# Attention and mixture of experts on one core: six of batch 1's ten k'q steps are called later, in pairs beside the first three expert blocks

## The chip, the cores and the metric

The kernel runs on one core of a Trainium2 chip. The core has five engines with a queue each, and each queue is worked off in order: PE (matrix multiply, with its weight loads shown as PEld), DVE (elementwise work of two operands, reductions), ACT (functions of one operand, casts, copies), POOL (here memsets, a few tensor operations and the scatters, which are DMAs that it issues itself) and SP (which issues the other DMAs). The metric is the time of one execution in device microseconds (us). Before the change it was 1244.78 us, the median of three runs from 1243.62 to 1246.61.

## The reference

There are B = 4 batches of N = 5056 tokens with C = 256 channels.

```python
qn = q / (norm(q, axis=1) + 1e-6)          # per channel, over all tokens of a batch
kn = k / (norm(k, axis=1) + 1e-6)
s = kn.T @ qn / tau                        # 256 x 256 for each batch
a = softmax(s)
x = v @ a                                  # 20224 tokens of 256 channels
logits = x @ w_gate + modality_bias[modality_id]
e = argmax(logits)                         # one of 8 experts for each token
out[token] = gate * (relu(x @ w1[e]) @ w2[e])   # hidden size 1024
```

So a batch's attention matrix needs a sum over all of its tokens (k'q and the squared norms) before the first of its tokens can be multiplied with it, and an expert can only start when enough tokens have been routed to it.

## The kernel before, in words

**Steps.** Each batch is cut into NS = 10 steps of 512 tokens (the last has 448), G = 40 steps in all, counted g = 0 to 39. Products in 32-bit floats are made from a high and a low part: ACT casts the high part, DVE subtracts to get the low part, and PE multiplies high by high, high by low and low by high.

**k'q** (`kq_pieces`, L218). A step of k'q has five pieces: load (L223), and for each half h of 256 tokens split (L250) and mm (L276). split makes two casts on ACT (L257) and two subtractions on DVE (L258), and for the norms a square on ACT (L272) and an addition to `acc` on DVE (L274), for q and for k. mm makes 4 matmuls of 512 columns (L283) and 4 of 256 (L287). A step that stands in `SELF` takes its norm from 4 more matmuls in each half (`selfk`, L294) in place of squares and additions. For batch 1's k these are steps 0 to 3 before the change.

**Routing** (`va_pieces`, L431). For step g: load of v (L443), transposes of v (L460) with their high and low parts (L464, L465), the product with the attention matrix (L476, copied out at L480), and `route` (L482): the logits, the largest of them, a running count of tokens for each expert (L507, L512 to L514), the row number `pi` of each token (L528), and four scatters of x into the sorted array `xs` (L407, on POOL). From g = 3 on `pick` (L556 to L581) chooses the rows and the expert of one block for each step; its result is `pki` (L579).

**Blocks** (`block_pieces`, L588). A block is 512 rows of one expert: SP reads `pki`, loads the weights (L615, L619, four DMAs of 512 KB) and the rows (`xr`, L596, which waits until the scatters of steps 0 to g have landed); ACT and DVE split the weights (L634, L635); PE transposes xr (L645) and makes the two layers (`hp`, L663, and `y`, L683). The block chosen after step g runs beside step g + 4. So steps g = 0 to 6 have no block beside them, the first block runs beside g = 7, and from then on each step has one.

**The order.** The loop at L768 calls, for each g, the pieces of up to three streams in turn (`_interleave`, L20): the block's, the routing's (with the next step's v, and the softmax ahead of a batch's first step), and the next batch's k'q, one step beside each g. The order in which pieces are called is a priority only: the framework then plans an order for each engine by its own estimate of the times, and may put an instruction ahead of others whose inputs come later. The trace shows how far: the memset of `modi` (L182) that is called after g = 15 runs at 95.99 us, amid the scatters of g = 2 and 3. What limits such moves is buffers. A tag of a pool has as many buffers as the pool says (p2: two, p3: three), and an instruction that needs one waits for the last use of the tile that had it.

**Buffers of k'q.** Inputs q and k have two buffers each in p2. Batch 1's steps 2, 3 and 4 borrow the three-deep buffers of the blocks' weights (`w1r`, `w2r`) as long as no block runs, the second halves of steps 0 to 3 borrow `xh` and `xl`, and their squares `hh` and `hl`.

Of the kernel before, what the change touches and what calls it, by code (L numbers as in the profile page):

```python
# [18 lines left out]

def _interleave(*streams):  # L20

    lists = [list(s) for s in streams if s]
    total = [len(x) for x in lists]
    at = [0] * len(lists)
    while any(a < n for a, n in zip(at, total)):
        i = min(
            (i for i in range(len(lists)) if at[i] < total[i]),
            key=lambda i: ((at[i] + 0.5) / total[i], i),
        )
        lists[i][at[i]]()  # L30
        at[i] += 1
# [3 lines left out]
def kernel(  # L35
# [20 lines left out]
    NS = -(-N // STEP)  # L56
# [15 lines left out]

    SELF = {
        "q": [{1, 4, 7}, set(), set(), set()],
        "k": [set(range(NS)), set(range(4)), set(), set()],
    }
    START = 3

    def parts(s):
        return P if s < NS - 1 else PL  # L80
# [137 lines left out]
    def kq_pieces(b, s):  # L218
        pp = parts(s)
        st = {}  # L220
        t0 = s * STEP

        def load():  # L223
            if s == 0:
                gram[b] = [
                    ps1.tile([P, 2 * C], F32, tag=f"{'y' if b == 0 else 'g'}{m}", name=f"g{m}_{b}")
                    for m in range(CH)
                ]
                acc[b] = p1.tile([P, 2, 2 * C], F32, tag="acc", name=f"acc_{b}", bufs=2)
                for n in ("k", "q"):  # L230
                    if SELF[n][b]:
                        selfp[n, b] = ps2.tile([P, CH, 2 * P], F32, tag="h", name=f"self{n}_{b}")
                        norm[n, b] = p1.tile([P, CH], F32, tag=f"n{n}", name=f"n{n}_{b}")
            for n, src, tag in (("q", q, "w1r"), ("k", k, "w2r")):
                if (b == 0 and s % 5 >= 2) or (b == 1 and 2 <= s < START + 2):
                    st[n] = p3.tile([P, TT, C], F32, tag=tag, name=f"{n}_{b}_{s}")
                else:
                    st[n] = p2.tile([P, TT, C], F32, tag=n, name=f"{n}_{b}_{s}")
                rows = src[b, t0 : t0 + pp * TT, :].rearrange("(p t) c -> p t c", t=TT)
                if b == 0 and s == 0:  # L240
                    st[n + "rows"] = rows
                else:
                    nc.sync.dma_start(st[n][:pp], rows)
            if b == 0 and s == 0:
                for h in range(2):
                    ts = slice(2 * h, 2 * h + 2)
                    for n in ("q", "k"):
                        nc.sync.dma_start(st[n][:, ts, :], st[n + "rows"][:, ts, :])

        def split(h):  # L250
            ts = slice(2 * h, 2 * h + 2)
            more = h == 1 and (b == 0 or (b == 1 and s < START + 1))
            qs = p2.tile([P, 2, 2 * C], F32R, tag="xh" if more else "qs", name=f"qs_{b}_{s}_{h}")
            ks = p2.tile([P, 2, 2 * C], F32R, tag="xl" if more else "ks", name=f"ks_{b}_{s}_{h}")
            st[h] = (qs, ks)
            for n, t in (("q", qs), ("k", ks)):
                nc.scalar.copy(t[:pp, :, 0:C], st[n][:pp, ts, :])  # L257
                nc.vector.tensor_tensor(  # L258
                    t[:pp, :, C : 2 * C], st[n][:pp, ts, :], t[:pp, :, 0:C].bitcast(F32), ALU.subtract
                )  # L260
            a = acc[b]
            for n, o in (("q", 0), ("k", C)):
                if s in SELF[n][b]:
                    continue
                first = h == 0 and s == min(set(range(NS)) - SELF[n][b])
                sq = a[:, :, o : o + C]
                if not first:
                    if b == 0 or (b == 1 and s < START + 1):
                        sq = p3.tile([P, 2, C], F32, tag="hh" if n == "q" else "hl", name=f"sq_{b}_{s}_{h}_{n}")
                    else:  # L270
                        sq = p2.tile([P, 2, C], F32, tag="sq", name=f"sq_{b}_{s}_{h}_{n}")
                nc.scalar.activation(sq[:pp], st[n][:pp, ts, :], AF.Square)  # L272
                if not first:
                    nc.vector.tensor_tensor(a[:pp, :, o : o + C], a[:pp, :, o : o + C], sq[:pp], ALU.add)  # L274

        def mm(h):  # L276
            qs, ks = st[h]
            for t in range(2):
                first = s == 0 and h == 0 and t == 0
                last = s == NS - 1 and h == 1 and t == 1  # L280
                for m in range(CH):
                    g = gram[b][m]
                    nc.tensor.matmul(  # L283
                        g, ks[:pp, t, m * P : (m + 1) * P], qs[:pp, t, :],
                        start=first, stop=False, skip_group_check=True,
                    )
                    nc.tensor.matmul(  # L287
                        g[:, 0:C], ks[:pp, t, C + m * P : C + (m + 1) * P], qs[:pp, t, 0:C],
                        start=False, stop=last, skip_group_check=True,
                    )  # L290
                    for n, x in (("k", ks), ("q", qs)):
                        mine = SELF[n][b]
                        if s in mine:
                            nc.tensor.matmul(  # L294
                                selfp[n, b][:, m, :], x[:pp, t, m * P : (m + 1) * P],
                                x[:pp, t, :].rearrange("p (s c) -> p s c", s=2)[:, :, m * P : (m + 1) * P],
                                start=s == min(mine) and h == 0 and t == 0 and m == 0,
                                stop=s == max(mine) and h == 1 and t == 1,
                                skip_group_check=True,
                            )  # L300
            for n in ("k", "q"):
                if h == 1 and SELF[n][b] and s == max(SELF[n][b]):

                    dg = p1.tile([P, 2 * P], F32, tag="sc", name=f"dg{n}_{b}", bufs=2)
                    for m in range(CH):
                        nc.vector.scalar_tensor_tensor(
                            dg, selfp[n, b][:, m, :], 1.0, ident12, ALU.mult, ALU.mult,
                            accum_out=norm[n, b][:, m : m + 1],
                        )

        yield load
        for h in range(2):
            yield lambda h=h: split(h)
            yield lambda h=h: mm(h)
# [110 lines left out]
    def slots_by(g):  # L425

        return max(0, g + 1 - START)

    first_block = LAG + START

# [314 lines left out]
    def once(blk, what):  # L745
        key = (blk["slot"], what)
        if key not in done:
            done.add(key)
            run(blk[what])
# [18 lines left out]
    for g in range(G):  # L768
        b, s = divmod(g, NS)
        streams = []  # L770
        for gg, blk in waiting:
            if gg <= g - LAG + 1:
                once(blk, "load")
        if len(waiting) > 0 and waiting[0][0] <= g - LAG:
            _, blk = waiting.pop(0)
            streams.append(block_stream(blk, waiting[0][1] if waiting and waiting[0][0] <= g - LAG + 1 else None))
        soft = list(softmax_pieces(b)) if s == 0 and b > 0 else []
        streams.append(soft + (va[g + 1][0] if g + 1 < G else []) + va[g][1])
        if b + 1 < B:
            streams.append(list(kq_pieces(b + 1, s)))  # L780
        _interleave(*streams)
        if waiting and waiting[0][0] <= g - LAG + 1:
            once(waiting[0][1], "load")
            once(waiting[0][1], "prep")
        if s == NS // 2 and b + 1 < B:
            setup_bias(b + 1)
        n = slots_by(g)
        while chosen < n:
            waiting.append((g, block_pieces(g, chosen, pick(g, chosen, False), False)))
            chosen += 1  # L790
# [42 lines left out]
    more = NB_MAX - NB_MIN + SHORT + slots_by(G - 1) - min(sure, slots_by(G - 1))  # L833
# [50 lines left out]
```

## Time and profile before

| | |
|---|---|
| median of three runs | 1244.78 us |
| the profiled execution's own time | 1245.85 us |
| its span, from the first instruction to the last | 1243.5 us |
| PE busy | 1221.7 us, 98% |
| DVE busy | 843.9 us, 68% |
| ACT busy | 754.1 us, 61% |
| POOL busy | 348.7 us, 28% |

All numbers of the trace come from the one profiled execution. Times with a point, such as 115.89, are microseconds from the start of its span. A PE that is shown busy is not a PE at its peak, since the ends of matmuls are modelled; how far apart they start says more. Shares over the whole span hide the stages: batch 0's k'q runs to about 50 us, then come softmax and routing without a block, then one block for each step, and after g = 39 blocks alone.

### The profile page before, as it was taken

To read this page: it belongs to the slowest core of one execution; us is meant where nothing else is said; L and a number is where in the kernel's file an instruction comes from. 1 tells how busy PE (TensorE), PEld (TensorE's weight loads), DVE (VectorE), ACT (ScalarE), POOL (GpSimd) and SP (SyncE) were. 2 spreads that over 40 slices of the span, in tenths; PEclk is the share of its full clock that TensorE was granted. 3 is DMA by queue.
4 is the path that set the end of the run, shared out by engine and by line. 5 is a ranking of instruction groups with operands and counts; after the bars stand their busy time and mean duration, and the time that the engine had idled before them with its cause. 6 is when DMAs were issued, how large, how long until landed. Compare 5 with 4: busy or idle time off the path is not lost.

```text
span 1243.5 us, 23786 instructions
## 1 busy us (share of the span) xinstructions
PE 1221.7 (98%) x8316; PEld 1116.2 (90%) x8316; DVE 843.9 (68%) x2215; ACT 754.1 (61%) x1531; POOL 348.7 (28%) x348
## 2 busy tenths in 40 slices
PE   8998999999999999999999999999999999999997
PEld 6897899999999999999999999999999999999997
DVE  7898967777777666866776776566655666665552
ACT  7885866666666666766666665565555555545553
POOL 0036343132222222322222222222332222321121
PEclk9998999999999999999999999999999999999999
DMA  9758864555555555555555554444554443467320
GB/s 322 252 191 282 271 205 151 161 190 186 176 170 172 178 171 171 162 176 170 170 181 186 175 167 136 136 134 143 164 173 154 149 153 121 147 211 219 119 95 28
DMA packets 113026, 215.06 MB, mean 173 GB/s; under 512 B 16128, under 2 KB 61696, under 8 KB 112896
## 3 DMA queue, kind: packets, MB, share of 16 engines
q1 hardware_dynamic: 97632, 171.84, 44.3%
q0 software_dynamic: 15264, 41.60, 8.8%
q8 instruction: 67, 1.10, 0.4%
q14 instruction: 63, 0.52, 0.1%
HBM read 167.06 MB, written 46.34 MB: 172 GB/s over the span
## 4 chain that ended last, share of the span: by engine, by line
PE 90%; DVE 3%; issue 3%; DMA 2%; ACT 1%; POOL 1%; SPq 0%; POOLq 0%; DVEq 0%; ACTq 0%
PE y L683 33%; PE hp L663 33%; PE xp L476 9%; PE g L283 5%; PE g L287 3%; PE vtp L460 3%; PE xtp L645 2%; DMA q<-in_q_dram 1%; PE selfk L294 1%; DVE acc L274 1%; POOL out_dram L407 1%; DMA xs<-x,pi 0%; PE ns L329 0%; DVE qs L258 0%; DVE w2l L635 0%
## 5 line engine op out<-in xcount | busy, mean ns | idle before, releaser
L683 PE MATMUL y<-w2h,hh 128*128 128x256 f32 x1264 | 356.7, 282 | 0.0
L407 POOL DMA_INDIRECT xs<-x,pi x160 | 173.0, 1081 | 647.8 <-ACT w1h L634 483.2
L683 PE MATMUL y<-w2l,hh 128*128 128x256 f32 x1264 | 352.7, 279 | 0.0
L683 PE MATMUL y<-w2h,hl 128*128 128x256 f32 x1264 | 351.4, 278 | 0.0
L669 DVE SCALAR_TENSOR_TENSOR hl<-hp,hh 128x512 fp32r<-128x512 f32 (+1 forms) x320 | 216.2, 676 | 147.0 <-ACT hh L668 146.8
L668 ACT ACTIVATE hh<-hp 128x512 fp32r<-128x512 f32 (+1 forms) x320 | 190.1, 594 | 169.2 <-PE hp L663 167.2
L663 PE MATMUL hp<-xh,w1h 128*128 128x512 f32 (+1 forms) x640 | 255.8, 400 | 0.3 <-ACT xh L650 0.3
L663 PE MATMUL hp<-xl,w1h 128*128 128x512 f32 (+1 forms) x640 | 250.3, 391 | 0.0
L663 PE MATMUL hp<-xh,w1l 128*128 128x512 f32 (+1 forms) x640 | 249.7, 390 | 0.0
L683 PEld LDWEIGHTS y<-w2h,hh 128*128 128x128 f32 x1264 | 237.5, 188 | 12.0 <-ACT yo L694 0.2
L683 PEld LDWEIGHTS y<-w2l,hh 128*128 128x128 f32 x1264 | 238.1, 188 | 10.0
L683 PEld LDWEIGHTS y<-w2h,hl 128*128 128x128 f32 x1264 | 236.6, 187 | 0.1
L407 POOL DMA_INDIRECT out_dram<-yo,xr x158 | 163.0, 1032 | 157.5 <-ACT yo L694 113.3
L635 DVE TENSOR_TENSOR w2l<-w2r,w2h 128x512 fp32r<-128x512 f32 x160 | 110.2, 689 | 71.9 <-ACT w2h L634 71.9
L635 DVE TENSOR_TENSOR w1l<-w1r,w1h 128x512 fp32r<-128x512 f32 x160 | 109.8, 686 | 55.5 <-ACT w1h L634 55.1
L634 ACT CAST w2h<-w2r 128x512 fp32r<-128x512 f32 x160 | 100.1, 625 | 74.9 <-PE y L683 67.4
L663 PEld LDWEIGHTS hp<-xh,w1l 128*128 128x128 f32 x640 | 120.1, 188 | 26.2
L634 ACT CAST w1h<-w1r 128x512 fp32r<-128x512 f32 x160 | 101.0, 631 | 60.0 <-PE hp L663 55.7
L663 PEld LDWEIGHTS hp<-xl,w1h 128*128 128x128 f32 x640 | 120.5, 188 | 14.1 <-DVE xl L651 0.4
L663 PEld LDWEIGHTS hp<-xh,w1h 128*128 128x128 f32 x640 | 120.1, 188 | 13.6 <-ACT xh L650 0.5
L283 PE MATMUL g<-qs,ks 128*128 128x512 f32 (+1 forms) x320 | 121.4, 402 | 5.7 <-ACT ks L257 5.7
L476 PE MATMUL xp<-ah,vh 128*128 128x264 f32 x320 | 96.9, 303 | 0.0
(152 smaller groups left out, 1833.0 us busy)
## 6 DMA issues: line engine op xcount, KB each, us to landing
w1r<-in_moe_w_dram SPq DMA_DIRECT2D x80, 512.0 KB, 3.5
w2r<-in_moe_w_dram SPq DMA_DIRECT2D x80, 512.0 KB, 3.7
xr<-xs SPq DMA_DIRECT2D x38, 516.0 KB, 4.7
v<-in_v_dram SPq DMA_DIRECT2D x36, 512.0 KB, 5.3
q<-in_q_dram SPq DMA_DIRECT2D x35, 512.0 KB, 7.5
k<-in_k_dram SPq DMA_DIRECT2D x35, 512.0 KB, 9.8
xs<-pad SPq DMA_DIRECT2D x9, 516.0 KB, 5.6
xs<-x,pi POOLq DMA_INDIRECT x160, 5.1
```

The lines of the kernel that those rows point to most:

```text
L283: nc.tensor.matmul(g, ks[:pp, t, m * P : (m + 1) * P], qs[:pp, t, :], start=first, stop=False, skip_group_check=True,)
L287: nc.tensor.matmul(g[:, 0:C], ks[:pp, t, C + m * P : C + (m + 1) * P], qs[:pp, t, 0:C], start=False, stop=last, skip_group_check=True,)
L407: ins = nc.gpsimd.indirect_dma_start(out=dst, out_offset=bass.IndirectOffsetOnAxis(ap=idx, axis=0), in_=rows, in_offset=None, bounds_check ...
L460: nc.tensor.matmul(tp[:, t * P : (t + 1) * P], st["v"][:, t, h * P : (h + 1) * P], ident, is_transpose=True, start=t == 0, stop=True, skip ...
L476: nc.tensor.matmul(xp[:, 0:DE], a[:, h, t * P : (t + 1) * P], w[:, h, :], start=i == 0, stop=i == len(seq) - 1,)
L634: nc.scalar.copy(hi, src)
L635: nc.vector.tensor_tensor(lo, src, hi.bitcast(F32), ALU.subtract)
L645: nc.tensor.matmul(tp[:, t * P : (t + 1) * P], st["xr"][:, t, h * P : (h + 1) * P], identr, is_transpose=True, start=t == 0, stop=True, sk ...
L663: nc.tensor.matmul(hp[:, 0:rows], w[:, h, fs], x[:, h, 0:rows], start=i == 0, stop=i == len(seq) - 1)
L668: nc.scalar.activation(hh[:, 0:rows], hp[:, 0:rows], AF.Relu)
L669: nc.vector.scalar_tensor_tensor(hl[:, 0:rows], hp[:, 0:rows], 0.0, hh[:, 0:rows].bitcast(F32), ALU.max, ALU.subtract)
L683: nc.tensor.matmul(y, a[:, tsl], w[:, j % 2, :], start=(j == 0 and i == 0 and t % 2 == 0), stop=(j == NJ - 1 and i == 2), skip_group_check ...
```

## The change

The diff does four things.

- A table `PLAN` says which steps of batch 1's k'q are called beside each step g of batch 0. Before, it was step g beside g. Now it is 0, 1 and 2 beside g = 0, 1 and 2, none beside g = 3, 4 and 5, step 3 beside g = 6, steps 4 and 5 beside g = 7, 6 and 7 beside g = 8, 8 and 9 beside g = 9. Later batches keep one step beside each g.
- Batch 1's k takes its norm from matmuls in steps 0 to 2, and no longer in step 3.
- The borrowed buffers go to batch 1's steps below `AHEAD` = 3 alone: `w1r` and `w2r` to step 2 (before: 2, 3 and 4), `xh`, `xl`, `hh` and `hl` to steps 0 to 2 (before: 0 to 3). Steps 3 and on use the two-deep buffers of their own.
- `_interleave` tests the length of a stream, since a stream can now be empty.

```diff
-    lists = [list(s) for s in streams if s]
+    lists = [list(s) for s in streams if len(s) > 0]
...
-        "k": [set(range(NS)), set(range(4)), set(), set()],
+        "k": [set(range(NS)), set(range(3)), set(), set()],
     }
     START = 3
+
+    PLAN = [[0], [1], [2], [], [], [], [3], [4, 5], [6, 7], [8, 9]]
+    AHEAD = 3
...
-                if (b == 0 and s % 5 >= 2) or (b == 1 and 2 <= s < START + 2):
+                if (b == 0 and s % 5 >= 2) or (b == 1 and 2 <= s < AHEAD):
                     st[n] = p3.tile([P, TT, C], F32, tag=tag, name=f"{n}_{b}_{s}")
...
-            more = h == 1 and (b == 0 or (b == 1 and s < START + 1))
+            more = h == 1 and (b == 0 or (b == 1 and s < AHEAD))
...
-                    if b == 0 or (b == 1 and s < START + 1):
+                    if b == 0 or (b == 1 and s < AHEAD):
                         sq = p3.tile([P, 2, C], F32, tag="hh" if n == "q" else "hl", name=f"sq_{b}_{s}_{h}_{n}")
...
         if b + 1 < B:
-            streams.append(list(kq_pieces(b + 1, s)))
+            steps = PLAN[s] if b == 0 else [s]
+            streams.append([f for i in steps for f in kq_pieces(b + 1, i)])
         _interleave(*streams)
```

## The prediction

> **What bounds the kernel now.** I began with the page and went on to the windows by stage, the waits and the chain around the first block, and the timelines of single queues. About 0.2%, or 2.5 us, is what a measurement of this kernel can tell from no change. The profiled execution took 1245.85 us, its span and 2.35 us around it; that is 1.07 us over the median of the three runs, so a difference found on it is taken off the median unchanged.
>
> ```profile
> span 1243.5 us, 23786 instructions
> ...
> PE 1221.7 (98%) x8316; PEld 1116.2 (90%) x8316; DVE 843.9 (68%) x2215; ACT 754.1 (61%) x1531; POOL 348.7 (28%) x348
> ```
>
> PE looks full over the whole span. The windows tell the stages apart; their columns are the window, busy us and instructions of each engine, the granted PE clock, the DMA share and GB/s.
>
> ```profile
> core 0: us, PE busy (x) PEld busy (x) DVE busy (x) ACT busy (x) POOL busy (x), PEclk, DMA share, GB/s
> 50.00:67.00 17.00, 15.86 (x111) 14.22 (x111) 13.84 (x38) 15.28 (x32) 0.00 (x0) 1.00 0.55 200
> 67.00:98.00 31.00, 30.84 (x236) 28.80 (x236) 30.25 (x117) 25.23 (x64) 14.66 (x16) 1.00 0.48 150
> 98.00:116.00 18.00, 12.95 (x79) 11.65 (x78) 12.45 (x59) 9.80 (x24) 13.23 (x12) 0.81 0.93 286
> 116.00:146.00 30.00, 29.10 (x191) 25.32 (x192) 28.21 (x76) 20.65 (x44) 7.02 (x8) 1.00 0.93 314
> 176.00:206.00 30.00, 30.00 (x207) 27.39 (x206) 22.12 (x56) 19.05 (x40) 10.28 (x11) 1.00 0.54 175
> ```
>
> From 146 on PE is the bound and nothing else is near it. From 67 to 98, where routing runs without a block, DVE is busy for 30.25 of 31 us. From 98 to 116 no engine is full: PE loses 5 us outright and gets 0.81 of its clock. So whatever the change wins, it wins before the first block; after it, matmuls count at the pace at which PE works them off. That pace is read from the chain, where runs of matmuls follow each other:
>
> ```profile
> 13.28 0.12 PE selfk L294
> ...
> 159.33 1.42 PE y L683 x12
> 160.75 0.73 PE xp L476 x6
> 161.48 1.40 PE hp L663 x6
> ```
>
> That is 0.117 us for 256 columns (1.40/12), 0.122 for 264 and 0.233 for 512. A step of k'q (8 matmuls of 512, 8 of 256) costs PE 8 x 0.35 = 2.8 us, a step's selfk 8 x 0.12 = 0.95 us.
>
> **What starts the first block.** Its first matmul, and what comes before it on three queues (start, us, engine):
>
> ```profile
> 115.89 0.73 PE L663 MATMUL hp<-xh,w1h 128*128 128x512 f32 x2 [0.33 <-ACT xh L650]
> ...
> 114.75 0.63 PE L645 MATMUL xtp<-identr,xr 128*128 128x128 f32 x6
> ...
> 109.29 0.35 SPq L596 DMA_DIRECT2D xr<-xs  x1
> ...
> 103.02 5.84 DMA xs<-x,pi
> ```
>
> ```profile
> 79.90 1.19 POOL L407 DMA_INDIRECT xs<-x,pi  x1 [34.73 <-ACT sq_q L272]
> 81.39 0.98 POOL L407 DMA_INDIRECT xs<-x,pi  x1 [0.30 <-issue]
> ...
> 94.64 1.38 POOL L407 DMA_INDIRECT xs<-x,pi  x1 [0.30 <-issue]
> 95.99 0.21 POOL L182 MEMSET modi<- 128x80 int32 x1
> ...
> 98.68 1.47 POOL L407 DMA_INDIRECT xs<-x,pi  x1 [0.16 <-DVE x L533]
> ...
> 103.02 0.97 POOL L407 DMA_INDIRECT xs<-x,pi  x1 [0.30 <-issue]
> ```
>
> The block's rows need the 16 scatters of g = 0 to 3. POOL issues one in 1.28 us (0.98 and 0.30) from 79.90 on, without a pause but for `modi` and three tensor operations, 2.7 us from 95.99 to 98.68. The sixteenth goes out at 103.02 and lands 5.84 later; xr is issued 0.43 after that, its transposes start 5.46 later, the first matmul 1.14 later: 115.89. The weights come just in time:
>
> ```profile
> SPq L186 <- POOL modi L182: 8.3, 1, 8.3
> ...
> PE rp L512 <- DVE pki L579: 4.1, 1, 4.1
> ACT w1h L634 <- DMA w1r<-in_moe_w_dram: 4.1, 1, 4.1
> ```
>
> ```profile
> 87.45 0.33 SPq L443 DMA_DIRECT2D v<-in_v_dram  x1
> 96.23 0.38 SPq L186 DMA_DIRECT2D modi<-in_moe_modality_id_dram  x1
> ...
> 98.88 0.41 SPq L615 DMA_DIRECT2D w1r<-in_moe_w_dram  x1
> ...
> 104.90 0.62 ACT L634 CAST w1h<-w1r 128x512 fp32r<-128x512 f32 x1 [4.11 <-DMA w1r<-in_moe_w_dram]
> ```
>
> SP stands 8.3 us before a load that needs POOL's memset, the weights leave at 98.88, and ACT stands before their cast until 104.90, with k'q casts of step 6 and all of DVE and PE behind it. None of this is a buffer of w1r: the change's earlier release of them wins nothing.
>
> **The change, part by part.** How much k'q stands before the block:
>
> ```profile
> L283 PE MATMUL g<-qs,ks 128*128 128x512 f32 x56 | 22.1, 412 | 0.0
> ...
> L294 PE MATMUL selfk<-ks 128*128 128x256 f32 x32 | 8.9, 292 | 0.0
> ```
>
> These are the groups from 50 to 115.8: 56/8 = 7 steps, 0 to 6. Steps 4, 5 and 6 now have a lower call place than the block's start, 3 x 2.8 = 8.4 us of PE. On DVE each has 8 operations of 0.60 us (4 L258, 4 L274):
>
> ```profile
> 91.27 0.60 DVE ks L258
> ...
> 92.06 0.60 DVE acc L274
> ```
>
> *Start of routing.* While g = 0's route runs, just ahead of its first scatter, DVE also makes these:
>
> ```profile
> 73.76 0.68 DVE L274 TENSOR_TENSOR acc<-acc,sq_q 128x512 f32<-128x512 f32 x1
> ...
> 78.16 0.68 DVE L274 TENSOR_TENSOR acc<-acc,sq_q 128x512 f32<-128x512 f32 x1
> ```
>
> There are four such additions from the one to the other, 2.4 us, which belong to steps 3 and 4 by their count. With the new places they yield to routing, but their inputs are still loaded early. Bounds 0 and 2.4 us; I take the middle, 1.2, since only the places change and the planner still fills holes: first scatter at 78.7.
>
> *POOL.* Fifteen scatters later, 78.7 + 15 x 1.28 = 97.9, if `modi` and its three operations come after them, else 100.6. I take 97.9: with fewer k'q instructions called before it, g = 3's route (DVE had it at 98.53, the x L533 above) is ready sooner, so POOL has no hole there. Then landing and load, by the page's medians:
>
> ```profile
> xr<-xs SPq DMA_DIRECT2D x38, 516.0 KB, 4.7
> ...
> xs<-x,pi POOLq DMA_INDIRECT x160, 5.1
> ```
>
> 97.9 + 5.1 + 0.43 + 4.7 + 0.5 + 1.14 = 109.8 for the block's first matmul, 6.1 us earlier (0.5 is what lies between landing and first transpose, 5.46 less about 5). Bounds: 107.6, with all 2.4 us and one us less in the DMAs, and 113.7, with no gain at the start and `modi` in the way.
>
> *Steps 4 to 6.* They cost nothing where PE waits anyway, 2.8 us each after the block has begun. Nearest are steps 0 to 2 of the same batch: called beside g = 0 to 2, they ran far ahead of it, in the softmax. But inputs now have two buffers, so step 5 waits for step 3's splits. DVE has room: 56.5 of 66 us busy before 116, less 14.4, plus 1.2, leaves 16 of 60 us free. I take two of the three as filled, one as paid: +2.8 us (bounds 0 and 8.4).
>
> *selfk of step 3* takes 0.95 us from PE and gives two squares to ACT and two additions (1.2 us) to DVE. Before the block PE is not the bound, and DVE has the room just counted: nothing (bounds -0.95 and +1.2). Without that room it is +1.2.
>
> *Pairs beside blocks.* A second step adds 8 x 0.60 = 4.8 us of DVE to 22.12 in a stretch that PE then fills for 32.8 us: hidden. In the first block's stretch DVE has 28.21 of 30 already, and 33.0 would stand against 32.8. I take nothing, since at 94% DVE PE still had 29.10 of 30; were it not covered, up to 4.8 us. Three q and three k loads (512 KB each) also move behind the first weights on SP's queue: at 314 GB/s some 10 us of transfers, in three stretches of which the later ones have a DMA share near 0.54. What is queued behind a late q on ACT are the casts of w1h, and PE behind those.
>
> Sum: -6.1 + 2.8 = **-3.3 us**: 1242.55 for the profiled execution, 1241.5 for the median.
>
> **A rule against it.** PE's hole and what came after:
>
> ```profile
> 103.00:107.00 4.00, 0.26 (x2) 0.00 (x0) 1.45 (x9) 2.10 (x5) 3.06 (x4) 0.87 0.99 337
> 107.00:110.00 3.00, 2.61 (x12) 2.30 (x13) 2.90 (x17) 2.20 (x5) 1.80 (x2) 0.50 1.01 374
> 110.00:113.00 3.00, 3.00 (x16) 2.93 (x15) 3.00 (x12) 2.62 (x7) 2.04 (x1) 0.53 0.87 186
> ```
>
> After 4 us of idling PE got half its clock for 6 us, 2.9 us of work lost. The Trainium skill, "TensorE: Matmul & The Clock Gate", section "HAM oscillation — how this bites in real kernels", says that no hole of PE should exceed some 3.4 us; the rows agree. Fewer matmuls ahead of the block make such a hole likelier there.
>
> **The rivals.**
> - *Slower: the weights set the start, and nothing fills.* If `modi`'s memset comes behind g = 3's scatters, SP is held until about 100 (97.9 + 1.3, and up to 1 us more where the route is late), the weights leave 2.65 later and land 6.0 after that, near 109; with three casts of 0.62 ahead of xh on ACT and the last 1.14 the first matmul comes near 112.5 (-3.4). ACT stands in their cast from 98, so none of steps 4 to 6 passes (+8.4): +5.0, 1249.8. For it: SP's 8.3 us and ACT's 4.1 us. Against: the memset waits only for a small DVE operation called after g = 5, now ahead of k'q. It decides if POOL gets to the memset after about 98.
> - *More: everything fills*, start at 107.6: -8.3, 1236.5. For it the 16 us of DVE; against it two buffers.
> - *Block earlier, steps later*: -6.1 with two steps paid, +5.6: -0.5, 1244.3.
> - *The hole before the block*: PE idles over 3 us there and the block begins at half clock: -3.3 + 2.9 = -0.4, 1244.4.
> - *The change doesn't do what it says*: the planner moved a memset from behind g = 15 to 96, and may put the steps where they were: 0, 1244.8.
>
> **How the numbers follow.** My forecast 0.42 (0.32 under 1242.3, 0.10 within the bound; its own range 1239 to 1244), everything fills 0.13, block earlier 0.08, hole 0.06, unchanged 0.08, slower 0.23. Faster 0.32 + 0.13 = 0.45, same 0.10 + 0.08 + 0.06 + 0.08 = 0.32, slower 0.23. The range runs from the case in which all fills to the slower one, 1236 to 1250.
>
> **What would show it.** The first L663 near 109.8 instead of 115.89; the first scatter before 79.90 and the sixteenth near 98; about 5 x 8 L283 before the first L663; an ACT wait for w1r under 4.1 us; PE busy 30 of 30 in the stretches after, with blocks one to three some 2.8 us longer. Wrong it is if the first L663 stays after 112, if the pairs leave holes in PE, or if DVE fills the first block's stretch.

## The result, and the profile after

The changed kernel takes **1252.99 us** (median of 4 runs, 1252.92 to 1255.24), beside 1245.09 us for the kernel before in the same runs: a ratio of 1.007, with an interval of 1.0057 to 1.0083. It is 7.9 us slower. The forecast was 1241.5, in a range of 1236 to 1250, and faster; the sign was wrong, and the time lies outside the range. Some experiments below also ran on two chips on which every kernel, the one before too (1283.54 and 1292.57 us), takes 3 to 4% longer for a reason that stays open; they are marked "long chip" and go by their ratio to the kernel before on the same chip.

All lines of the code after `PLAN` have moved down by 3: L663 of before is L666 now, L283 is L286, L407 is L410, L512 is L515. From the page of the kernel after:

```profile
span 1250.7 us, 23781 instructions
...
PE 1223.3 (98%) x8308; PEld 1116.6 (89%) x8308; DVE 843.6 (67%) x2217; ACT 754.8 (60%) x1533; POOL 348.4 (28%) x348
```

The engines do the same work as before (PE 1223.3 us against 1221.7); it is spread over 7.2 us more of span. The windows by stage, in the columns of the prediction:

```profile
50.00:67.00 17.00, 15.91 (x111) 14.18 (x111) 13.84 (x40) 14.69 (x31) 0.09 (x1) 1.00 0.56 199
67.00:98.00 31.00, 29.87 (x232) 27.20 (x231) 29.87 (x143) 22.57 (x61) 17.01 (x18) 1.00 0.58 165
98.00:116.00 18.00, 8.78 (x43) 7.68 (x44) 10.08 (x39) 9.03 (x20) 11.78 (x12) 0.74 0.84 286
116.00:146.00 30.00, 28.26 (x183) 24.75 (x182) 24.47 (x58) 18.40 (x37) 6.98 (x6) 0.99 0.78 258
146.00:176.00 30.00, 30.00 (x206) 27.62 (x205) 22.31 (x53) 20.97 (x43) 8.28 (x8) 1.00 0.64 207
176.00:206.00 30.00, 29.43 (x198) 26.53 (x197) 21.21 (x53) 20.38 (x41) 8.60 (x8) 1.00 0.60 193
```

From 98 to 116 PE does 8.78 us of work where it did 12.95, at a granted clock of 0.74 where it had 0.81. That is the stretch in which steps 4 to 6 were to have been done. How many were, the groups of PE show, up to the first block (36 matmuls of 512 columns, where the kernel before had 56):

```profile
L286 PE MATMUL g<-qs,ks 128*128 128x512 f32 x36 | 14.3, 414 | 0.0
```

At 8 a step these are steps 0 to 3 and half of step 4; before it was 0 to 6. The waits from 85 to 122 show what PE did instead (line waited for: us in total, times, longest):

```profile
DVE w1l L638 <- ACT w1h L637: 7.6, 2, 7.0
ACT x L483 <- DMA xs<-x,pi: 7.0, 1, 7.0
...
PE xp L479 <- ACT x L483: 6.2, 1, 6.2
...
PE rp L515 <- DVE sm L535: 3.5, 1, 3.5
```

PE stands for 6.2 us and again for 3.5. The order of ACT's queue tells why for the first (start, us, engine; the releaser in brackets), with the chain's row for the transfer ahead of it:

```profile
95.31 7.28 DMA xs<-x,pi
```

```profile
102.69 0.38 ACT L483 COPY x<-xp 128x264 f32<-128x264 f32 x1 [6.99 <-DMA xs<-x,pi]
102.97 0.62 ACT L260 CAST qs<-q 128x512 fp32r<-128x512 f32 x1
103.49 0.62 ACT L260 CAST ks<-k 128x512 fp32r<-128x512 f32 x1
104.85 0.38 ACT L483 COPY x<-xp 128x264 f32<-128x264 f32 x1 [0.74 <-PE xp L479]
105.12 0.62 ACT L637 CAST w1h<-w1r 128x512 fp32r<-128x512 f32 x1
```

The copy of x for a step far ahead needs a buffer whose scatter, sent out at 95.31, lands 7.28 us later. The casts of k'q and of the weights stand behind that copy in ACT's queue, DVE's subtractions behind the casts (7.0 us), PE behind both. PE then works at half pace: `xp` matmuls of 264 columns follow each other at 0.22 us from 103.51 on, and at 0.12 from 106.58. The second hole is what had piled up: in it ACT and DVE are busy throughout (3.70 and 3.67 of 3.70 us).

```profile
108.30:112.00 3.70, 0.23 (x2) 0.00 (x0) 3.67 (x18) 3.70 (x10) 2.78 (x4) 1.00 0.71 218
```

The start of the block itself, in the order of the prediction's rows:

```profile
80.47 1.16 POOL L410 DMA_INDIRECT xs<-x,pi  x1 [8.52 <-DVE oh L502]
...
100.99 0.97 POOL L410 DMA_INDIRECT xs<-x,pi  x1 [0.31 <-issue]
```

```profile
93.95 0.41 SPq L618 DMA_DIRECT2D w1r<-in_moe_w_dram  x1
...
107.03 0.35 SPq L599 DMA_DIRECT2D xr<-xs  x1
```

```profile
112.13 0.41 PE L648 MATMUL xtp<-identr,xr 128*128 128x128 f32 x3
...
113.79 0.80 PE L666 MATMUL hp<-xh,w1h 128*128 128x512 f32 x1 [0.34 <-ACT xh L653]
```

The block starts at 113.79 instead of 115.89. From the first matmuls of the blocks, read off the timelines, and the count of 512-column k'q matmuls between them:

| | before | after | before, again | after, again |
|---|---|---|---|---|
| 512-column k'q ahead of block 1 | 56 | 36 | 56 | 36 |
| start of block 1, us | 115.9 | 113.8 | 116.9 | 114.9 |
| stretches of blocks 1, 2, 3, us | 30.5, 29.8, 29.8 | 33.7, 33.5, 34.0 | 29.2, 29.8, 29.8 | 32.8, 33.3, 34.2 |
| k'q matmuls in them | 8, 8, 8 | 12, 16, 16 | 8, 8, 8 | 12, 16, 16 |
| stretch of block 4, us | 33.6 | 33.4 | 33.6 | 33.4 |
| start of block 5, us | 239.7 | 248.3 | 239.3 | 248.5 |

A stretch with one step takes 29.8 us, so without any 27.0 are due (29.8 - 2.8). Stretches that did run without a step took 27.1, 28.0 and twice 28.2 in the experiments below, so 27.0 is the low end. The sum of the two profiles: the start -2.1; 20 matmuls more behind it, 20 x 0.35 = +7.0; what the three stretches take beyond 27.0 and 0.35 a matmul, 4.8 against 0.7, +4.0; the fourth stretch -0.3: +8.6 at the start of block 5 (248.3 - 239.7). That stays to the last block; the tail behind it is 1.5 us shorter, and the span 7.2 us longer. The last two columns are two profiles taken beside each other on another chip: -2.0 + 7.0 + 4.5 - 0.3 = +9.2, a tail shorter by 0.1, and spans of 1241.6 and 1250.8 us. The same three terms, each within 0.5 us.

### The profile page after: what moved, and what is told of

Its sections match the earlier page's. It is cut to its first block, busy times and chain, and to the rows that moved or that the text cites. A ratio compares the mean times of both kernels' runs of the same rounds, so it can differ in the third digit from the quotient of the medians.

```text
span 1250.7 us, 23781 instructions
## 1 busy us (share of the span) xinstructions
PE 1223.3 (98%) x8308; PEld 1116.6 (89%) x8308; DVE 843.6 (67%) x2217; ACT 754.8 (60%) x1533; POOL 348.4 (28%) x348
## 4 chain that ended last, share of the span: by engine, by line
PE 88%; DVE 3%; DMA 3%; issue 3%; ACT 2%; POOL 1%; SPq 0%; POOLq 0%; DVEq 0%; ACTq 0%
PE hp L666 33%; PE y L686 33%; PE xp L479 8%; PE g L286 5%; PE g L290 3%; PE vtp L463 2%; PE xtp L648 2%; DMA k<-in_k_dram 1%; DVE acc L277 1%; DMA xs<-x,pi 1%; DMA q<-in_q_dram 1%; PE selfk L297 1%; POOL out_dram L410 1%; PE ns L332 0%; DVE ks L261 0%
## 5 line engine op out<-in xcount | busy, mean ns | idle before, releaser
L410 POOL DMA_INDIRECT xs<-x,pi x160 | 171.6, 1073 | 643.4 <-ACT w1h L637 468.5
L666 PE MATMUL hp<-xh,w1h 128*128 128x512 f32 (+1 forms) x640 | 256.5, 401 | 0.3 <-ACT xh L653 0.3
L666 PE MATMUL hp<-xl,w1h 128*128 128x512 f32 (+1 forms) x640 | 250.5, 392 | 0.0
L666 PE MATMUL hp<-xh,w1l 128*128 128x512 f32 (+1 forms) x640 | 250.1, 391 | 0.0
L410 POOL DMA_INDIRECT out_dram<-yo,xr x158 | 162.5, 1029 | 157.5 <-ACT yo L697 113.9
L666 PEld LDWEIGHTS hp<-xh,w1l 128*128 128x128 f32 x640 | 120.3, 188 | 26.2
L666 PEld LDWEIGHTS hp<-xl,w1h 128*128 128x128 f32 x640 | 120.9, 189 | 13.8
L666 PEld LDWEIGHTS hp<-xh,w1h 128*128 128x128 f32 x640 | 120.5, 188 | 13.6 <-ACT xh L653 0.5
L286 PE MATMUL g<-qs,ks 128*128 128x512 f32 (+1 forms) x320 | 121.4, 403 | 5.5 <-ACT ks L260 5.5
```

The source lines that it names most:

```text
L286: nc.tensor.matmul(g, ks[:pp, t, m * P : (m + 1) * P], qs[:pp, t, :], start=first, stop=False, skip_group_check=True,)
L410: ins = nc.gpsimd.indirect_dma_start(out=dst, out_offset=bass.IndirectOffsetOnAxis(ap=idx, axis=0), in_=rows, in_offset=None, bounds_check ...
L666: nc.tensor.matmul(hp[:, 0:rows], w[:, h, fs], x[:, h, 0:rows], start=i == 0, stop=i == len(seq) - 1)
```

## The experiments

Several experiments give a time beside the kernel before as it ran on the same chip (1245.6 to 1245.9 us, where nothing else is said). "Ahead" is the number of batch 1's 512-column k'q matmuls in front of the first block, "start" its first matmul.

**Is it the call places, or the buffer of x?** A spare buffer for one more x takes away the wait of 7.0 us.

```diff
-            more = g % 2 == 1 and g + 2 < first_block
+            more = g % 2 == 1 and g + 1 < first_block
```

> The changed kernel, with x of step g = 5 in a buffer of xr, so that x of g = 6 finds one free and ACT's 7.0 us wait for a scatter of g = 2 should go. Theory A (call place): the steps of k'q called beside blocks are planned behind the block's start and cost PE 2.8 us each, 2.5 of them here; the hole is only where PE waits for a start that POOL and the DMAs set. Then the first L666 stays within 1 us of 113.8 and the time within 1.5 us of the changed kernel's 1253. Theory B (buffer of x): the wait on ACT keeps the steps from running ahead; then 4 to 7 us come back, 1246 to 1249.

1253.17 us, ratio 1.0052 (1.0035 to 1.0069); ahead 36, start 113.6, stretches 33.9, 34.0 and 34.5. The waits from 85 to 122:

```profile
PE rp L515 <- DVE sm L535: 7.9, 1, 7.9
...
ACT w1h L637 <- DMA w1r<-in_moe_w_dram: 3.7, 2, 2.9
DVE w1l L638 <- ACT w1h L637: 3.2, 2, 2.1
```

The wait is gone and the hole is not: it went from two pieces to one of 7.9 us, now behind the weights' casts and subtractions. The buffer of x was the stopper that came first, not the cause.

**Norms and buffers alone**, one step beside each g as before:

```diff
-    PLAN = [[0], [1], [2], [], [], [], [3], [4, 5], [6, 7], [8, 9]]
+    PLAN = [[s] for s in range(NS)]
```

> The changed kernel with one step beside each g, as before: only the norm of k's step 3 and the borrowed buffers stay changed. Theory A: within 1.5 us of before (1245), with 7 steps ahead of the first block. Rival C (the smaller input buffers or the norm cost the time): 1249 or more, with fewer than 7 steps ahead of the block.

1244.57 us, ratio 0.9987 (0.9977 to 0.9996); ahead 56, start 113.4. So the fewer borrowed buffers and step 3's norm cost nothing, and the start is early with them alone; the loss comes with the call places. A second measurement, on a long chip:

> Edit: the norms and borrowed buffers of the change alone, one step of k'q beside each g as before (a second measurement). If its gain is one of the kernel: ratio 0.998 to 0.9995 with an interval below 1, 1244.6 us beside 1245.9. If it was chance: the interval holds 1.

Ratio 1.0007 (0.9978 to 1.0036). The gain isn't settled; by the medians it is under 0.2% in either.

**The places alone**, on the norms and buffers of before:

```diff
-        "k": [set(range(NS)), set(range(3)), set(), set()],
+        "k": [set(range(NS)), set(range(4)), set(), set()],
...
-                if (b == 0 and s % 5 >= 2) or (b == 1 and 2 <= s < AHEAD):
+                if (b == 0 and s % 5 >= 2) or (b == 1 and 2 <= s < AHEAD + 2):
...
-            more = h == 1 and (b == 0 or (b == 1 and s < AHEAD))
+            more = h == 1 and (b == 0 or (b == 1 and s < AHEAD + 1))
...
-                    if b == 0 or (b == 1 and s < AHEAD):
+                    if b == 0 or (b == 1 and s < AHEAD + 1):
```

> The table of call places alone, a second time, since in the first all kernels were 3% slower, the kernel before too (1283.5 us). Theory A (call place): 5 to 9 us over before, first matmul of a block between 113 and 117, 32 to 36 matmuls of 512 columns of k'q ahead of it. If it is more than 10 us over before, the borrowed weight buffers beside the blocks cost as well.

1257.76 us, ratio 1.0089 (1.0063 to 1.0114); ahead 32, start 119.7, stretches 31.4, 34.5 and 34.6. Alone the places lose 11.9 us, more than the whole change. By the expectation's own mark (more than 10 us) the buffers of before cost as well beside the new places: half a step fewer is ahead, and the start is 6 us later. Step 3's q goes out at 105.21, behind xr (104.81), and PE works the step's 8 matmuls off between xr's transposes and the block, from 114.14 on; why its q goes out so late is not shown.

```profile
114.14 1.22 PE L286 MATMUL g<-qs,ks 128*128 128x512 f32 x2 [3.23 <-ACT ks L260]
```

(On a long chip its ratio was 1.0167, 1.0117 to 1.0218.)

**What steps 4 to 6 are worth.** From the kernel before, and then from the changed one, these three steps are left out; batch 1's attention matrix is then of seven steps' tokens.

```diff
-                first = h == 0 and s == min(set(range(NS)) - SELF[n][b])
+                first = h == 0 and s == min(set(range(NS)) - SELF[n][b] - ({4, 5, 6} if b == 1 else set()))
...
-            streams.append(list(kq_pieces(b + 1, s)))
+            streams.append([] if b == 0 and s in (4, 5, 6) else list(kq_pieces(b + 1, s)))
```

> The kernel before, with steps 4, 5 and 6 of batch 1's k'q left out (loads, splits, matmuls, squares), so 8.4 us less PE work. Theory A: all three were hidden ahead of a start that the scatters set: 0 to 2.5 us less, first L663 at 113 or later. Rival D (their DVE and ACT work sets the start): 5 to 8 us less, first L663 at 108 to 111.

1240.55 us, ratio 0.9959 (0.9947 to 0.9971); ahead 40, start 115.4: step 7 moves ahead into the room (the second form, with 112 rows, is batch 0's last step, which still runs at 50 us and is not counted). The first stretch then has no step and takes 27.1 us.

```profile
L283 PE MATMUL g<-qs,ks 128*128 128x512 f32 x40 | 15.7, 404 | 0.0
L283 PE MATMUL g<-qs,ks 112*128 112x512 f32 x2 | 0.8, 393 | 0.0
```

The time is rival D's, the start theory A's. Without 8.4 us of PE's work, of which step 7 fills 2.8 again, the start moves by 0.5 us (1.6 from that of the other profile of the kernel before). The rest comes from behind it: in the profiles 3.4 us from the first stretch and 2.0 from the tail, which is 1.5 longer in this profile of the kernel before than in the other. So the k'q that stands ahead of the block in the kernel before delays it by 1.6 us at most, where 5.6 us of it are gone.

```diff
-    PLAN = [[0], [1], [2], [], [], [], [3], [4, 5], [6, 7], [8, 9]]
+    PLAN = [[0], [1], [2], [], [], [], [3], [], [7], [8, 9]]
```

> The changed kernel, with the same three steps left out. Theory A: 2.5 of the three were paid beside the blocks, so 7 us less, and with the lighter pairs up to 9: 1244 to 1246, the same as the kernel before without them within 2 us, first L666 at about 113. Theory B: 3 us less at most, 1250.

1244.63 us, ratio 0.9986 (0.9976 to 0.9996), 8.4 us under the changed kernel; ahead 34, start 115.3, stretches 28.0, 29.3 and, with the pair 8 and 9, 34.1 where 27.0 + 5.6 = 32.6 were due. Leaving the steps out is worth 8.4 us here and 5.4 there. Up to the fourth block it is 8.2: 22 matmuls fewer in the stretches are 7.7, what these lose beyond them is 2.0 less, and the start is 1.5 later. So the work moved behind the start is paid; that the sum comes to 3 x 2.8 us is chance. The two kernels without the steps are 4.1 us apart, not within the 2 us expected: their starts are the same, and the stretches with pairs make the difference. The pair keeps 1.5 us of its own.

**One, not two, behind the start.** Steps 3 to 6 all beside g = 6, so that no pair stands beside a block:

```diff
-    PLAN = [[0], [1], [2], [], [], [], [3], [4, 5], [6, 7], [8, 9]]
+    PLAN = [[0], [1], [2], [], [], [], [3, 4, 5, 6], [7], [8], [9]]
```

> Steps 3 to 6 all beside g = 6, no pairs, a second time. In the first, all kernels were 3% slower; there 56 matmuls came ahead of the block and the ratio was 1.006. Theory A: as 7 steps are ahead, within 2.5 us of before, less what its later start costs. Rival F: 4 to 7 us over before.

1248.11 us, ratio 1.0016 (1.0005 to 1.0027); ahead 56, stretches 28.7, 30.7 and 29.8 with 8 matmuls in each, and no cost beside the blocks (-0.2 us in all). But the start is 120.3, though xr goes out at 106.13. The timeline in between:

```profile
106.13 0.35 SPq L599 DMA_DIRECT2D xr<-xs  x1
...
106.59 0.39 SPq L246 DMA_DIRECT2D q<-in_q_dram  x1
...
111.22 0.84 PE L648 MATMUL xtp<-identr,xr 128*128 128x128 f32 x8 [0.65 <-DMA xr<-xs]
112.43 0.62 ACT L260 CAST qs<-q 128x512 fp32r<-128x512 f32 x1 [1.44 <-DMA q<-in_q_dram]
...
115.01 1.22 PE L286 MATMUL g<-qs,ks 128*128 128x512 f32 x2 [2.94 <-DVE qs L261]
...
120.29 0.43 PE L666 MATMUL hp<-xh,w1h 128*128 128x512 f32 x1
```

The last of the steps called ahead has its q loaded behind xr on SP. PE transposes xr at 111.22, waits 2.94 us for that step's subtraction, and works the step off at half clock before it turns to the block. This is the other side of the place: a step called ahead whose inputs come after the block's own rows holds the block back.

**One more step ahead**, on the kernel before, and on the norms and buffers of the change:

```diff
-    lists = [list(s) for s in streams if s]
+    lists = [list(s) for s in streams if len(s) > 0]
...
-            streams.append(list(kq_pieces(b + 1, s)))
+            steps = [[0], [1], [2], [3], [4], [5, 6], [7], [8], [9], []][s] if b == 0 else [s]
+            streams.append([f for i in steps for f in kq_pieces(b + 1, i)])
```

> The kernel before with the steps from 6 on called one place earlier, a second time. Theory A: 60 to 64 matmuls of 512 columns ahead of the block, start by 117, 1 to 3 us less than before. Rival D: the start 2 to 5 us later and no gain, 0 to 3 us over before.

> The earlier places with the changed kernel's norm and borrowed buffers, a second time (ratio 0.9993 in the first, slower by 3% for all). Theory A: 2 to 4 us less than before, 1241 to 1243 where before is 1245. Rival D: 0 to 3 us over before.

1249.91 us, ratio 1.003 (1.0019 to 1.0041), ahead 60, start 120.1; and 1246.63, ratio 1.0005 (0.9992 to 1.0018), ahead 62, start 120.2. More k'q ahead, less behind the start, and no gain: the start came late in both, with 4 and 6 k'q matmuls of 512 columns between the transposes of xr and the block's first. (On a long chip these two and the one with all steps beside g = 6 had ratios of 1.0064, 0.9993 and 1.0062: the same order.)

**One step moved, one pair**, with the norms and buffers of the change:

```diff
-    PLAN = [[0], [1], [2], [], [], [], [3], [4, 5], [6, 7], [8, 9]]
+    PLAN = [[0], [1], [2], [3], [4], [5], [], [6, 7], [8], [9]]
```

> Edit: the norms and buffers of the change, with PLAN one step beside each g from 0 to 5, none beside g = 6, steps 6 and 7 beside g = 7, 8 beside g = 8, 9 beside g = 9: one step moved behind the start of the first block, one pair. Theory 'a moved step is paid with PE's 2.8 us and a pair adds 1.2 to 1.6 us': about 48 of the 512-column matmuls ahead of the block instead of 56, first stretch 27.0 + 5.6 + 1.4 = 34.0, time 2.8 to 4.4 us over the same kernel without the move, 1247.4 to 1249. Rival 'one step fits in the holes, only three do not': step 7 or part of it moves ahead of the block in its place, 52 to 56 such matmuls, time 1244.5 to 1246.

On a long chip: ratio 0.9969 (0.9943 to 0.9994), 52 ahead. Again on another chip:

> The kernel with one step moved and one pair, a second time (1290.67 beside 1292.57, ratio 0.997, where all kernels ran 4% longer). Theory 'one step fits in the holes': 54 to 56 of the 512-column matmuls ahead of the block, all of the first three stretches within 1 us of 30, time 1243.5 to 1245.5 where the kernel before takes 1245.9. Rival 'a moved step is paid': 48 ahead, 1247.4 to 1249.

1244.49 us, ratio 0.9994 (0.9985 to 1.0003).

```profile
L286 PE MATMUL g<-qs,ks 128*128 128x512 f32 x52 | 20.2, 406 | 0.0
```

Neither side held whole. Half of the moved step (4 of 8 matmuls) went ahead of its place, as the prediction thought of two steps in three; the other half was paid in the first stretch, 32.7 us for 12 matmuls, 1.5 more than 27.0 + 4.2. With a start at 113.2 it comes out where the kernel before does. So filling held for half of one moved step; with the places beside g = 3, 4 and 5 empty it held for half of one step in three.

**As many ahead, but single steps beside the first two blocks:**

```diff
-    PLAN = [[0], [1], [2], [], [], [], [3], [4, 5], [6, 7], [8, 9]]
+    PLAN = [[0], [1], [2], [], [], [], [3], [4], [5], [6, 7, 8, 9]]
```

> Edit: the changed kernel with PLAN ending [3], [4], [5], [6, 7, 8, 9]: as many steps called before the block as after the change, but one step (not two) beside g = 7 and g = 8, and four beside g = 9. Theory 'each pair leaves a hole of its own' (1.2 to 1.6 us beyond 2.8 us a step): the first two stretches of blocks near 27.0 + 2.8 = 29.8 us plus at most 0.5, the third 27.0 + 4 x 2.8 = 38.2 plus 2 to 3 for its crowd; the start of the fourth block 1 to 3 us earlier than after the change (215.0), time 1250 to 1252. Rival 'the extra 4.1 us come from being late as a whole (buffers and loads that trail the start), however the steps are spread': the fourth block starts within 0.5 us of 215.0 and the time is 1252.5 to 1253.5.

Ratio 1.0091 (1.0062 to 1.012), on a long chip, so its stretches are measured from its own start: ahead 36; 29.5 us with 4 matmuls, 29.8 with 8, 42.8 with 32. The first loses 1.1 us, the second nothing, the last 4.6. From its first block to its fourth it takes 102.1 us, where the changed kernel takes 101.2 and 100.3. So the loss lies where steps crowd, as the one theory had it, but it is not saved by crowding them elsewhere, as that theory also had it.

**Does the start belong to the kernel?** Starts of 113 to 116 and of 120 had come from two chips, so both kernels were profiled beside each other on a third.

> The kernel before once more, profiled on the chip of the two runs beside it. The first block's start came at 113 to 116 us in some experiments and at 120 in four that ran together on another chip. Theory 'the start belongs to the kernel': 115.9 within 1 us here, whatever the chip. Rival 'the start differs by chip or by execution': another start by 3 us or more, and the kernel after, beside it, later by as much. Time 1245 to 1246 if the chip is like the first.

> The changed kernel once more beside the kernel before. Theory 'work paid and pairs': 36 to 40 of the 512-column matmuls ahead of the block, start within 2.5 us of that of the kernel before in its profile beside it, the first three stretches 33 to 34.5 us, ratio 1.005 to 1.009. Rival 'the late start carries it': the start 3 us or more apart from the kernel before.

1245.84 us and 1253.58 us, the second at a ratio of 1.0065 (1.0051 to 1.0079); starts 116.9 and 114.9. Between these two chips the start of a kernel moves by 1.0 and 1.1 us. The chip of the four starts at 120 was not profiled with the kernel before, but there xr's transposes began at 109.7 to 114.8, no later than elsewhere (111.8 to 115.7), and what is late comes behind them. On the long chip the start does move: norms and buffers alone began at 121.0 for 113.4, and the kernel with one pair at 121.9 for 113.2. The waits of the second, from 85 to 122, are those of the first profile:

```profile
DVE w1l L638 <- ACT w1h L637: 7.8, 2, 7.2
ACT x L483 <- DMA xs<-x,pi: 7.2, 1, 7.2
```

## Why the prediction was wrong

**What bounds the kernel** held: PE after 146, and no engine between 98 and 116. So did the rule of counting: a step that PE works off behind the start costs 8 x 0.35 = 2.8 us (a stretch takes 29.8 us with one step, and 27.1 to 28.2 without).

**The start** was forecast at 109.8 and came at 113.79, -2.1 where -6.1 stood in the sum; the middle of the bounds was taken, and the far one, 113.7, was measured, though not by the terms that the bound was made of. Its terms: the first scatter 78.7, measured 80.47 (+1.8: routing did not begin earlier, and k'q's additions did not yield to it: five of them run from 72.42 to 78.72, where four ran from 73.76 to 78.16); fifteen more at 1.28 should have ended at 19.2 us, and took 20.52 (+1.3, single ones of 1.05 to 1.54 instead of 0.98); from the sixteenth to xr 5.53, took 6.04 (+0.5); to the transposes 5.2, took 5.10; to the first matmul 1.14, took 1.66 (+0.5: two `rp` matmuls stand in between). `modi` was judged rightly: it no longer stands amid the scatters, and the weights go out at 93.95 instead of 98.88.

```profile
78.72 0.68 DVE L277 TENSOR_TENSOR acc<-acc,sq_q 128x512 f32<-128x512 f32 x1
```

**Steps 4 to 6** are the step that failed. "I take two of the three as filled, one as paid: +2.8 us (bounds 0 and 8.4)": 2.5 of the three were paid, +7.0. The reasoning was that steps 0 to 2 run far ahead of their place and that DVE has 16 of 60 us free. The room was there: DVE is busy 10.08 us of 18 from 98 to 116, PE 8.78. It could not be used, because room in an engine is not room in its queue. With k'q called later, routing and the weights of the block were planned ahead of it, ran up against the scatters' buffers, and stood at the head of ACT's and DVE's queues, with the casts of k'q behind them. With the wait for the buffer taken away the next one took its place (7.9 us), and with the places of before, on the same buffers, 56 matmuls went ahead and the start stayed (113.4). So it's the places. The two-deep inputs that the prediction feared come in only behind them: steps 4 and 5 were loaded in time (the last of their squares runs at 87.61), while step 6's q goes out after the block has begun, once step 4's last subtraction (112.74) is done, and its k at 126.59.

```profile
117.49 0.35 SPq L246 DMA_DIRECT2D q<-in_q_dram  x1
```

That the heads of the queues, and not some other effect of the places, kept 2.5 steps back is read from these rows; no run changed the order of one queue alone.

**Pairs beside blocks** were taken at nothing and cost 4.0 us (4.5 in the second pair of profiles). DVE did not run out: 24.47, 22.31 and 21.21 us of 30, under the 28.21 of the first such window before. The bound of 4.8 us stood in the prediction for another reason. What the waits of PE show is small and in many places; from the first stretch, and then the second and the third:

```profile
PE xp L479 <- ACT x L483: 0.9, 1, 0.9
PE rp L515 <- DVE sm L534: 0.8, 1, 0.8
```

```profile
PE rp L515 <- DVE oh L502: 0.5, 1, 0.5
```

```profile
PE rp L515 <- DVE oh L502: 0.8, 1, 0.8
```

The first is a late load, as the prediction's last sentence on the pairs feared, but of k, with the copy of x behind it. SP sends k out behind w1r; ACT's square of k waits for it:

```profile
126.59 6.37 DMA k<-in_k_dram
```

```profile
132.99 0.63 ACT L275 ACTIVATE sq_k<-k 128x512 f32<-128x512 f32 x1 [2.70 <-DMA k<-in_k_dram]
```

The others are routing's chain on DVE. In the third stretch its first operation (L488) stands behind an addition and two subtractions of k'q and the block's `xl`, and `rp` on PE, with the block's matmuls behind it, waits for the chain's end:

```profile
205.89 0.69 DVE L277 TENSOR_TENSOR acc<-acc,sq_k 128x512 f32<-128x512 f32 x1
206.49 0.69 DVE L261 TENSOR_TENSOR qs<-q,qs 128x512 fp32r<-128x512 f32 x1
207.09 0.69 DVE L654 TENSOR_TENSOR xl<-xtp,xh 128x512 fp32r<-128x512 f32 x1
207.69 0.69 DVE L261 TENSOR_TENSOR ks<-k,ks 128x512 fp32r<-128x512 f32 x1
208.29 0.19 DVE L488 TENSOR_TENSOR L<-x,bsel 128x32 f32<-128x32 f32 x1
...
210.90 0.19 PE L515 MATMUL rp<-oh,trim 112*128 112x32 bf16 x1 [0.79 <-DVE oh L502]
```

Together the waits named for PE are 3.0 us; in the first stretch the block's start at a reduced clock adds to them. That these are all of the 4.0 is argued, not shown. The loss goes with the crowding, but not with it alone: the second and third stretches with 16 matmuls took 33.3 to 34.6 us in every profile off the long chips, where 32.6 are due, 32 in one lost 4.6, and 8 in each lost nothing in all with steps 3 to 6 all beside g = 6. But the kernel before with the steps from 6 on one place earlier took 32.0 us for a stretch with 8 and 28.2 for one with none.

**selfk** at nothing held as far as the runs can tell: it is part of the norms and buffers, which measured 0.9987 and 1.0007.

**The rivals.** The slower one came closest: 1249.8 by "nothing fills", where 2.5 of 3 steps did not. Its reason was not what happened: it had the weights late behind `modi`, and they were early. What it had right is ACT standing in one instruction with k'q behind it. *The hole before the block* came true too, 6.2 and 3.5 us, with half clock after it (from 115.45 to 116.73 the block's matmuls of 512 columns stand 0.43 us apart instead of 0.233). The Trainium skill, "TensorE: Matmul & The Clock Gate", section "HAM oscillation — how this bites in real kernels", says that PE should have no idle gap over some 3.4 us. After the hole of 6.16 us the `xp` matmuls stand 0.22 us apart, against 0.12 later, which agrees. The prediction priced these rivals one by one. They are one event, since the hole is the time in which nothing fills, and together with the pairs' 4.0 us they lead to 1253.

**By its own marks:** "wrong it is if the first L663 stays after 112, if the pairs leave holes in PE": both happened. The count to watch was given as about 40 ahead of the block, and 36 were there; but 40 is two steps fewer than the 56 of before, while the sum had one paid, which is 48. With its own mark in the sum the forecast would have been -6.1 + 5.6 = -0.5.

## What to carry to other kernels

Work that lies under a stretch bound by something else (here 16 scatters at 1.28 us and their landing) is free only there: before it is moved out, count what it will cost where PE is the bound, here 2.8 us a step, and ask what holds if the start's gain comes out at its far bound, as it did here. Room in an engine's busy share is no evidence that work will move into it: look for what will stand at the head of its queue, because where an earlier call place puts other work in front, the first missing buffer or late load stops all that is behind. Two background steps beside one block cost 0.7 to 2.0 us more than the sum of their matmuls in the second and third stretches here, even with DVE busy for 71 to 82% of the changed kernel's windows, and a step called ahead whose inputs are loaded behind the block's own rows delays the block (120.3 us here, where kernels without such a step began at 113.2 to 116.9 off the long chips).

## What was not expected of the hardware

The scatters, all of one form, have a median of 4.1 us from issue to landing in this profile. One took 2.66 us from 91.47 and another 7.28 from 95.31, just after the first loads of the weights (93.95 to 95.69) went out; the DMA share from 96.7 to 103 is 1.03. That the weights slow the scatter is argued, not shown; the estimate by medians was short here (5.53 us from the sixteenth scatter to xr, 6.04 measured).

```profile
91.47 2.66 DMA xs<-x,pi
95.31 7.28 DMA xs<-x,pi
```
